# Two moves in a polysketch-attention and ELU-MLP kernel: a rounding step placed inside a division, and GpSimd's weight sums split over two steps

## The chip, the cores and the metric

The kernel runs on one core of one Trainium2 chip. The metric is device time in microseconds (us) of that core, lower is better. All numbers before the change come from three timed runs and from one more execution that the hardware profiler recorded.

## The reference, cut to what matters

Attention with a polynomial feature map feeds a two-layer block with an ELU between its layers.

```python
# q, k, v: (4, 4, 1088, 32); S1, S2: (8, 32); w_in: (128, 2048); w_out: (2048, 128)
def phi(x):                                   # 64 features from two sketches of 8
    a = einsum('rd,bhsd->bhsr', S1, x)
    b = einsum('rd,bhsd->bhsr', S2, x)
    return einsum('bhsi,bhsj->bhsij', a, b).reshape(..., 64)
kv  = einsum('bhsf,bhsd->bhfd', phi(k), v)
z   = sum(phi(k), axis=2)
num = einsum('bhsf,bhfd->bhsd', phi(q), kv)
den = einsum('bhsf,bhf->bhs', phi(q), z)[..., None] + 1e-06
x   = (num / den).transpose(0, 2, 1, 3).reshape(4352, 128)
h   = x @ w_in
g   = where(h > 0, h, exp(min(h, 0)) - 1)
out = g @ w_out
```

q, k and v arrive as 32-bit floats, S1, S2, w_in and w_out as 64-bit floats; of these the kernel reads each number as two 32-bit words and makes a 32-bit float itself.

## The kernel before, in words

**Tiling.** The 4352 rows of x are cut into 9 groups of at most 512 rows (`g`, 0 to 8; the last has 256). The 2048 hidden columns are cut into 8 blocks (`cp`, 0 to 7) of 256. One step is one pair (g, cp): TensorE multiplies block cp of w_in by the group (`mm1`), ScalarE and VectorE make the ELU of it in two halves (`elu`, tile `gg`), and two steps later TensorE multiplies the result by block cp of w_out. The list `steps` fixes the order: steps 0 to 13 go through groups 0 and 1 for the first blocks and end with blocks 6 and 7 of group 0; steps 14 and 15 are blocks 6 and 7 of group 1; from step 16 on, one group after another takes all eight blocks.

**Seven products instead of eight.** From step 14 on (`seven`), the product with w_out uses seven block products in place of eight. This needs sums of quarters of `gg` (`sums7`, tile `tt`, lines 751 to 756, four GpSimd instructions a step) and sums of quarters of w_out (`weights7`, tile `SS`, line 740, four GpSimd instructions for a range of blocks). `mm2_seven` (line 792) issues the matmuls; in each step its first products need `gg` alone, and the third kind, named `p6`, needs `tt` of line 755 and `SS`.

**The order of work** is written out by hand, engine by engine: each engine runs its instructions in the order of the program text. The lists `at`, `mid` and `late` put a piece of work into a step: after its `mm1`, between the two halves of the ELU, or at its end.

**Rounding of weights.** A block of weights goes through five steps: `RA` (line 101, VectorE, masks the upper word into `W`), `RB` (line 106, ScalarE), `RS` and `RM` (lines 116 and 120, VectorE), `RD` (line 128) and `RE` (line 136). `RA(0)` and `RA(1)` are the first steps for blocks 0 and 1 of w_in, whose data come by DMA from SyncE's queue (line 173).

**The first group's division.** Before the first step stands a start-up sequence. For group 0, `q2_den` computes the denominators and divides: a product (line 603, tile `pw`), a sum over eight terms (line 608, `den`), a reciprocal (line 609) and a product with it (line 611, `an`). Its argument `between` is a function that is called after the first of these. `q2_out` then forms the 64 features in two halves (line 624, `qp`), with `RA(1)` between them. TensorE transposes these halves (`q4_early`, line 636, `qtp`), and multiplies by kv (`q5_early`, line 643, `xps`); ScalarE copies the result to `xg` (line 649), on which the first `mm1` waits.

```python
    def q2_den(g, zq=None, between=None):
        ...
            nc.vector.tensor_mul(pw...)          # line 603
        if between:
            between()
        den = work.tile([P, 8 * H], F32, name="den", tag="den")
        nc.vector.tensor_reduce(den[:, :m], pw[:, :m], axis=AX, op=ADD)   # line 608
```

GpSimd at that time builds small tables for later groups (`make_Sxp`, `make_SWq`, `Z_share`: lines 312 to 318 and 454).

Of the kernel before, what the change touches and what calls it, by code (L numbers as in the profile page):

```python
# [22 lines left out]
def _ap(ap: bass.AP, free):  # L23
    return dataclasses.replace(ap, ap=[list(ap.ap[0])] + [list(x) for x in free])
# [3 lines left out]
def kernel(  # L28
# [28 lines left out]
    NP = NC // 2  # L57
# [120 lines left out]
    def round_w(f, i, *a):  # L178
        if wide:
            cp, w_in, w_out = order[i]  # L180
            c = slice(0 if w_in else 2 * P, 4 * P if w_out else 2 * P)
            f(raw_w[cp][:, c], W[:, cp, c], *a)

    def RA(i):
        round_w(round_a, i)
# [337 lines left out]
    def q1z_first():  # L523
        p = psum.tile([P, 512], F32, name="zqp", tag="h", bufs=4)
        for i in range(4):
            for u in range(2):
                b, t = half_tile(0, 2 * i + u)
                nc.tensor.matmul(p[64 * u:64 * u + 64, i * 32:i * 32 + 32].rearrange("p (h r) -> p h r", h=H),
                                 qT[b][:, t, :], SW[:, :, 2, :], skip_group_check=True, tile_position=(0, 64 * u))
        return p[:, :128].rearrange("p (t h r) -> p h t r", t=4, h=H)  # L530
# [65 lines left out]
    def q2_den(g, zq=None, between=None):  # L596
        m = H * (un[g] if g > 1 else qn[g])
        x = abw[g][:, :m, :]
        pw = pws[g % 2]
        if zq is None:  # L600
            nc.vector.tensor_mul(pw[:, :m, :R], x[:, :, R:2 * R], x[:, :, 2 * R:3 * R])
        else:
            nc.vector.tensor_mul(pw[:, :m, :R].rearrange("p (h t) r -> p h t r", h=H),
                                 x[:, :, R:2 * R].rearrange("p (h t) r -> p h t r", h=H), zq)
# [3 lines that stand above are left out]
        nc.vector.tensor_reduce(den[:, :m], pw[:, :m], axis=AX, op=ADD)  # L608
        nc.vector.reciprocal(den[:, :m], den[:, :m])
        an = work.tile([P, 8 * H, R], F32, name="an", tag="an")  # L610
        nc.vector.tensor_mul(an[:, :m], x[:, :, R:2 * R], _ap(den[:, :m], [[1, m], [0, R]]))
        ans[g] = an

    def q2_out(g, parts=1, between=None):
        m = H * qn[g]
        x, an = abw.pop(g), ans.pop(g)
        qp[g] = work.tile([P, 4 * H, R, R], F32, name="qp", tag="qp", bufs=2)
        for i in range(parts):
            if i and between:
                between()  # L620
            h = slice(i * m // parts, (i + 1) * m // parts)
            a_ = an[:, h]
            b_ = x[:, h, :R]
            nc.vector.tensor_mul(qp[g][:, h], _ap(a_, list(a_.ap[1:]) + [[0, R]]),
                                 _ap(b_, [b_.ap[1], [0, R], b_.ap[2]]))
# [337 lines left out]
    KO_first(7, KT)  # L963
    keep_warm(1, 96, 64)
    zq = q1z_first()
    q2_den(0, zq)
    RA(0)
    q2_out(0, 2, lambda: RA(1))
    KA(0)
    KS_first()  # L970
# [53 lines left out]
    def late(n, f, *a):  # L1024
        extra.setdefault((n, 1), []).append((f, *a))
# [75 lines left out]
    late(60, q4, 8)  # L1101

    late(12, weights7, slice(NP - 2, NP))
    late(15, weights7, slice(0, NP - 2))

    N = len(steps)
    for n in range(2, N):
# [95 lines left out]
```

## Time and profile before

| what | value |
|---|---|
| timed runs | 265.53, 265.70, 265.88 us; median 265.70 us |
| profiled execution, device time | 266.02 us |
| its span, first to last instruction | 264.2 us |
| TensorE busy | 258.6 us, 98% of the span |
| VectorE busy | 188.2 us, 71% |
| ScalarE busy | 184.5 us, 70% |
| GpSimd busy | 167.3 us, 63% |
| granted TensorE clock | full speed in all 40 slices |

The profile calls TensorE PE (its weight loads PEld), VectorE DVE, ScalarE ACT, GpSimd POOL and SyncE SP. L740 is line 740 of the kernel. Times are counted from the start of the span. Around the span lie 1.8 us that the profiled execution's device time has beyond it.

### The profile page before, as it was taken

The numbers are of one execution on the slowest core, as the hardware profiler recorded it, in microseconds if no ns is written. First come the engines' busy times: TensorE is split into PE (matmuls) and PEld (weight loads), VectorE is DVE, ScalarE is ACT, GpSimd is POOL, SyncE is SP. The second block draws the span as 40 slices with busy tenths as digits, with TensorE's granted clock in tenths as the row PEclk, the third lists the DMA queues.
The fourth block names the chain that finished last, engine by engine and source line by source line (L and its number), as shares of the span: only waits on it lengthen the run. The fifth ranks groups of instructions, "written<-read, shape, count | busy, mean of one in ns | idle before, by whom it ended". The sixth has DMA issues, their size and how long they took to land.

```text
span 264.2 us, 9735 instructions
## 1 busy us (share of the span) xinstructions
PE 258.6 (98%) x4127; PEld 160.7 (61%) x4127; DVE 188.2 (71%) x349; ACT 184.5 (70%) x356; POOL 167.3 (63%) x247
## 2 busy tenths in 40 slices
PE   8899999999999999999999999999999999999994
PEld 6652334354346666667666666665766666667994
DVE  6799999997969997996567675644446445674651
ACT  2469978677567556785587777776777777777792
POOL 4400009103279996798858799898688888997310
PEclk9999999999999999999999999999999999999999
DMA  6996089010011110001100110011001100110021
GB/s 183 342 347 200 0 254 241 12 55 35 2 22 25 23 24 2 2 4 20 28 3 0 26 20 0 2 15 29 3 2 20 23 4 0 17 17 10 2 32 30
DMA packets 26442, 13.73 MB, mean 52 GB/s; under 512 B 19328, under 2 KB 24576, under 8 KB 26400
## 3 DMA queue, kind: packets, MB, share of 16 engines
q1 hardware_dynamic: 25968, 12.76, 18.8%
q8 instruction: 32, 0.52, 0.9%
q10 hardware_dynamic: 368, 0.30, 0.3%
q14 instruction: 10, 0.08, 0.1%
q0 software_dynamic: 64, 0.07, 0.1%
HBM read 10.88 MB, written 2.23 MB: 50 GB/s over the span
## 4 chain that ended last, share of the span: by engine, by line
PE 96%; POOL 1%; DVE 1%; ACT 1%; issue 0%
PE h L257 44%; PE pb L792 16%; PE pa L792 13%; PE o L257 5%; PE pb L768 4%; PE ol L257 3%; PE idle L265 1%; PE kv L428 1%; PE h L686 1%; PE qps L686 1%; POOL kp L324 1%; PE kfps L360 1%; PE qps L576 1%; PE qtp L636 1%; PE kv L257 1%; PE abp L341 1%
## 5 line engine op out<-in xcount | busy, mean ns | idle before, releaser
L257 PE MATMUL h<-xg,W 128*32 128x512 f32 (+3 forms) x904 | 130.7, 539 | 0.3 <-ACT xg L649 0.3
L875 DVE SCALAR_TENSOR_TENSOR gg<-e,h 128x512 f32<-128x512 f32 x128 | 85.6, 682 | 54.1 <-ACT e L869 50.6
L867 ACT ACTIVATE e<-h 128x512 f32<-128x512 f32 x128 | 75.5, 590 | 45.8 <-PE h L257 44.0
L869 ACT ACTIVATE e<-e 128x512 f32<-128x512 f32 x128 | 80.9, 632 | 3.8
L257 PEld LDWEIGHTS h<-xg,W 128*32 128x32 f32 (+1 forms) x904 | 42.6, 122 | 43.1 <-issue 35.5
L754 POOL TENSOR_TENSOR tt<-gg 128x256 f32<-128x256 f32 x50 | 37.0, 741 | 15.3 <-DVE gg L875 14.9
L751 POOL TENSOR_TENSOR tt<-gg 128x256 f32<-128x256 f32 x50 | 36.7, 734 | 7.7 <-DVE gg L875 7.3
L755 POOL TENSOR_TENSOR tt<-tt,gg 128x256 f32<-128x256 f32 x50 | 37.5, 751 | 3.9
L756 POOL TENSOR_TENSOR tt<-gg,tt 128x256 f32<-128x256 f32 x50 | 37.2, 744 | 3.9
L792 PEld LDWEIGHTS pa<-gg,W 128*64 128x64 f32 (+1 forms) x496 | 23.8, 125 | 23.5 <-issue 22.9
L792 PE MATMUL pa<-gg,W 128*64 128x128 f32 (+1 forms) x496 | 30.5, 274 | 0.0
L792 PE MATMUL pb<-tt,SS 128*64 128x128 f32 (+1 forms) x480 | 29.5, 273 | 0.0
L792 PEld LDWEIGHTS pb<-tt,SS 128*64 128x64 f32 (+1 forms) x480 | 22.7, 126 | 0.0
L792 PE MATMUL pa<-tt,SS 128*32 128x128 f32 (+1 forms) x288 | 21.1, 273 | 0.0
L792 PE MATMUL pb<-gg,SS 128*64 128x128 f32 (+1 forms) x256 | 19.8, 273 | 0.0
L792 PE MATMUL pb<-tt,W 128*64 128x128 f32 (+1 forms) x256 | 19.8, 273 | 0.0
L133 POOL TENSOR_TENSOR raw<-raw,tiny 128x512 f32<-128x512 f32 x1 | 1.0, 1047 | 29.5 <-DVE raw L128 29.5
L257 PE MATMUL o<-gg,W 128*32 128x512 f32 x128 | 15.3, 594 | 0.0
L792 PEld LDWEIGHTS pa<-tt,SS 128*32 128x32 f32 (+1 forms) x288 | 13.5, 123 | 0.3 <-POOL tt L755 0.3
L792 PEld LDWEIGHTS pb<-gg,SS 128*64 128x64 f32 (+1 forms) x256 | 12.6, 125 | 0.0
L792 PEld LDWEIGHTS pb<-tt,W 128*64 128x64 f32 (+1 forms) x256 | 12.6, 125 | 0.0
L768 PE MATMUL pb<-gg,W 128*32 128x256 f32 x192 | 11.6, 380 | 0.0
(163 smaller groups left out, 279.5 us busy)
## 6 DMA issues: line engine op xcount, KB each, us to landing
raw<-in_moe_w_in_dram SPq DMA_DIRECT2D x8, 256.0 KB, 6.1
raw<-in_moe_w_out_dram SPq DMA_DIRECT2D x8, 256.0 KB, 6.0
hd_k<-in_k_dram SPq DMA_DIRECT2D x3, 544.0 KB, 7.2
hd_q<-in_q_dram SPq DMA_DIRECT2D x3, 544.0 KB, 8.6
out_dram<-ob SPq DMA_DIRECT2D x88, 16.0 KB, 1.5
v<-in_v_dram SPq DMA_DIRECT2D x4, 288.0 KB, 7.5
v<-in_v_dram SPq DMA_DIRECT2D x4, 256.0 KB, 8.4
hd_k<-in_k_dram SPq DMA_DIRECT2D x1, 288.0 KB, 3.3
```

What stands on the lines that cost most here:

```text
L257: nc.tensor.matmul(dst[c:c + tile], lhs[:, c:c + tile], rhs, skip_group_check=True, tile_position=(0, c), **kw)
L265: nc.tensor.matmul(idle[c:c + tile, :cols], ones[:, :tile], ones[:, :cols], skip_group_check=True, tile_position=(0, c))
L686: nc.tensor.matmul(ps[w][s * r:s * r + s, 64 * k:64 * (k + m)], lhs, qpT[g, i][rows, o + 2 * k:o + 2 * (k + m), f, :], start=(f == 0 and j ...
L751: nc.gpsimd.tensor_tensor(t[:, 0], b12, b11, op=SUB)
L754: nc.gpsimd.tensor_tensor(t[:, 2], b22, b12, op=SUB)
L755: nc.gpsimd.tensor_tensor(t[:, 1], t[:, 2], b11, op=ADD)
L756: nc.gpsimd.tensor_tensor(t[:, 3], b21, t[:, 1], op=SUB)
L768: nc.tensor.matmul(acc[1][0][r:r + width[0], 256 * hi:256 * hi + 256], lhs[:, w:w + width[0]], gg[:, c, 256 * u:256 * u + 256], start=(cp ...
L792: nc.tensor.matmul(bank[r:r + width[0], P * col:P * col + P], lhs[:, w:w + width[0]], rhs[:, u], start=(first and i in ((0,) if g == 1 els ...
L867: nc.scalar.activation(e, hs[g, cp][c][:, :n], RELU, scale=-1.0)
L869: nc.scalar.activation(e, e, EXP, scale=-1.0)
L875: nc.vector.scalar_tensor_tensor(gs[g, cp][:, c, :n], es[g, cp][:, c, :n], -1.0, hs[g, cp][c][:, :n], op0=ADD, op1=MAX)
```

## The change

The first step of rounding block 0 of w_in, `RA(0)`, is issued inside `q2_den` of group 0, between line 603 and line 608, in place of after line 611. The sums of w_out blocks 0 to 5, which were all made at the end of step 15, are made in two parts: blocks 0 to 2 at the end of step 13, and blocks 3 to 5 at the end of step 15. The values computed are the same.

```diff
     zq = q1z_first()
-    q2_den(0, zq)
-    RA(0)
+    q2_den(0, zq, lambda: RA(0))
     q2_out(0, 2, lambda: RA(1))
...
     late(12, weights7, slice(NP - 2, NP))
-    late(15, weights7, slice(0, NP - 2))
+    late(13, weights7, slice(0, 3))
+    late(15, weights7, slice(3, NP - 2))
```

## The prediction

> **What bounds the kernel now.** I read the busy shares first, then the chain that ended last.
>
> ```profile
> PE 258.6 (98%) x4127; PEld 160.7 (61%) x4127; DVE 188.2 (71%) x349; ACT 184.5 (70%) x356; POOL 167.3 (63%) x247
> PE 96%; POOL 1%; DVE 1%; ACT 1%; issue 0%
> ```
>
> TensorE carries 96% of the chain. An edit on VectorE or GpSimd can only shorten the start-up, before the first mm1 (16.1 us), or one of the few moments when TensorE waits later. So I looked for both. The chain in order of time, around the first step that uses w_out sums of block 0 (step 18 multiplies what step 16 made, group 2, block 0):
>
> ```profile
> 84.14 0.44 PE pa L792 x16
> 84.58 0.01 issue
> 84.59 0.43 PE pa L792 x8
> 85.02 0.87 PE pb L792 x32
> ```
>
> Columns: start, length, what. Eight such matmuls take 0.22 us elsewhere (0.44 for 16 in the first line), and these took 0.43: the 56 of the step took 1.75 us from 84.14 to 85.89, against 1.53 us in the step before (80.89 to 82.42). TensorE stood for **0.2 us**. The table of waits names the releaser (total us, times, longest):
>
> ```profile
> PEld pa L792 <- POOL tt L755: 0.3, 1, 0.3
> ```
>
> GpSimd's own order of time shows why it was late:
>
> ```profile
> 64.66 0.46 POOL L740 TENSOR_TENSOR SS<-W,SS 128x128 f32<-128x128 f32 x1
> 69.75 0.73 POOL L751 TENSOR_TENSOR tt<-gg 128x256 f32<-128x256 f32 x1 [4.62 <-DVE gg L875]
> ...
> 78.29 1.02 POOL L740 TENSOR_TENSOR SS<-W 128x384 f32<-128x384 f32 x1
> 79.39 1.01 POOL L740 TENSOR_TENSOR SS<-SS,W 128x384 f32<-128x384 f32 x1
> 80.35 1.02 POOL L740 TENSOR_TENSOR SS<-W 128x384 f32<-128x384 f32 x1
> 81.33 1.01 POOL L740 TENSOR_TENSOR SS<-W,SS 128x384 f32<-128x384 f32 x1
> 82.31 0.73 POOL L751 TENSOR_TENSOR tt<-gg 128x256 f32<-128x256 f32 x1
> 83.00 0.72 POOL L754 TENSOR_TENSOR tt<-gg 128x256 f32<-128x256 f32 x1
> 83.80 0.73 POOL L755 TENSOR_TENSOR tt<-tt,gg 128x256 f32<-128x256 f32 x1
> ```
>
> The four w_out sums hold GpSimd from 78.29 to 82.31. The ELU that line 751 reads was there at 78.06 (VectorE, 77.37 + 0.69), and its second half at 79.21. Line 755 ends at 84.53; TensorE goes on at 84.59. Before, GpSimd had 4.6 idle us, from 65.1 to 69.75.
>
> In the start-up, VectorE's order of time:
>
> ```profile
> 10.12 0.29 DVE L603 TENSOR_TENSOR pw<-abq,zqp 128x128 f32<-128x128 f32 x1 [0.23 <-PE zqp L528]
> 10.51 0.30 DVE L608 TENSOR_REDUCE den<-pw 128x16 f32<-128x144 f32 x1
> 10.84 0.25 DVE L609 RECIPROCAL den<-den 128x16 f32<-128x16 f32 x1
> 11.13 0.29 DVE L611 TENSOR_TENSOR an<-abq,den 128x128 f32<-128x128 f32 x1
> 11.34 0.29 DVE L101 TENSOR_SCALAR W<-raw 128x256 uint32<-128x256 uint32 x1
> 11.54 0.68 DVE L624 TENSOR_TENSOR qp<-an,abq 128x512 f32<-128x512 f32 x1
> 12.14 0.28 DVE L101 TENSOR_SCALAR W<-raw 128x256 uint32<-128x256 uint32 x1
> 12.34 0.68 DVE L624 TENSOR_TENSOR qp<-an,abq 128x512 f32<-128x512 f32 x1
> ```
>
> An instruction that needs the one ahead starts about 0.03 us after its end (10.81 to 10.84); one that doesn't starts before that end (11.34 against 11.42). The second half of qp releases TensorE (transposes at 13.17, 0.14 us after), and the chain then runs through PE and ACT to mm1 without a gap. So what VectorE gains here counts in full.
>
> **What the Trainium skill says.** "SBUF — State Buffer", section "Who interferes with whom": VectorE and GpSimd share a pair of SBUF ports under an exclusive lock. A tensor_scalar in its two-port mode takes it, a VectorE instruction with two SBUF inputs contends with a GpSimd one that reads, a reduce never does; the later one waits out the earlier. The trace agrees: at 45.72 line 120 took 2.07 us instead of 0.43, ending 0.29 after GpSimd's line 324 ended (47.50); at 43.99 line 116, two inputs, took 1.69 instead of 0.69. "VectorE: DVE Perf Modes", section "Mode 2×_2P": tensor_scalar gets two results a cycle even on 32-bit data. Line 101 agrees: 0.29 us for 256 elements, 0.43 for 512, so 0.55 ns an element, against 1.05 for two-input products (0.29 for 128, 0.68 for 512). RA(0) is thus an instruction that takes the lock.
>
> **Part 1, RA(0) into the division.** Removed between lines 611 and 624: their starts are 0.41 us apart. In group 2, without a step between, they are 0.32 apart (67.52 to 67.84), so the gain is 0.09. Added between 603 and 608: group 1 already has such a step there (RA(2)), and its starts are 16.20, 16.40 and 16.60, that is 0.40 apart; group 0 shows 0.39 today without it. The cost is 0.01. Net on paper **-0.08 us**.
>
> The lock takes part of it back. RA(0) will start near 10.33. GpSimd then runs the four copies of line 318 (9.85 to 10.51) and line 454 (10.46 to 10.68); at 11.34 it was idle. The nearest row is line 109 at 2.95: a tiny tensor_scalar beside GpSimd's copy of line 269 took 0.29 instead of 0.17 and ended 0.04 after the copy (3.20). With the rest of 256 elements at 0.55 ns, RA(0) held by the last copy ends at 10.51 + 0.04 + 0.12 = 10.67 instead of 10.62: +0.05. Bounds: 0 if it gets in first; if line 454 gets in first, 10.68 + 0.16 = 10.84, +0.22. I take +0.05, as line 116 got the lock between two GpSimd instructions (45.1). Part 1: **-0.03 us**, between -0.08 and +0.14.
>
> RA(0) also waits for its DMA. That was issued at 3.89 and landed 5.4 us later, at 9.3, 1.0 us before the new place: no wait. If the data came after 10.33, line 608 and all of the division behind it would wait that long. RB(0) on ACT gains nothing: it stands behind the copy at 11.89. No DMA is moved, and SP's queue keeps its order.
>
> **Part 2, the split sums.** One block is 64 columns. A line-740 instruction takes 0.46 us for 128 columns and 1.02 for 384, so about 0.60 for 192. By start-to-start times, interpolated, the four take 0.68 + 0.55 + 0.55 + 0.57 = 2.35 us (the 384-wide ones take 4.02). Four instructions are added in all: GpSimd does 0.7 us more. At the end of step 13 its first four run from 65.12, behind the sums of blocks 6 and 7, to about 67.5; nothing of GpSimd is queued behind them until line 751 at 69.75. Cost nothing, covered by the idle 4.6 us; without that cover it would be 2.35 us of GpSimd.
>
> At the end of step 15, GpSimd is free at 78.29 + 2.35 = 80.64 instead of 82.31, and line 755 ends near 82.9. TensorE wants it at 84.39 (its first 16 products start at 83.95 and take 0.44). The stall of **0.2 us goes**, with 1.5 us to spare. What is late next: line 755 for the following step ended at 87.56, wanted at 89.2, so nothing. From 82.4 to 102 TensorE is busy 19.59 of 19.60 us, and the steps there take 1.53 to 1.56 us apart from the switches after other matmuls: no second stall to win.
>
> The lock again: lines 601 (66.58), 611 (67.52) and 666 (67.84) of group 2's division have two SBUF inputs and now meet GpSimd. Line 601 falls into the third sum and may wait 0.3, line 611 perhaps 0.1; by 67.9 GpSimd is through. Line 673, which follows, ends at 70.82, and TensorE takes its result at 71.75: 0.93 us of slack covers it.
>
> **Sum.** -0.20 - 0.03 = -0.23 us on the profiled execution (span 264.2, device time 266.02; the 1.8 around it unchanged). That execution lies 0.32 above the median; from the median 265.70 it gives **265.5 us** (265.47), or -0.09%. A measurement of this kernel can tell about 0.2%, 0.53 us, from no change; so I forecast no change that counts.
>
> **Rivals.** (a) *The stall is larger without the profiler, or in most executions.* One more lock lost by GpSimd before 84.5 costs it what line 755 lost at 92.92 (1.60 instead of 0.73), near 0.8 us, and then the sum of the gains is 0.2 + 0.8 + 0.03 = 1.0: 264.7. For it: GpSimd is busy without a gap from 78 to 102. Against: in this stretch VectorE has one SBUF input in nearly everything, and all three runs agree within 0.35 us. (b) *Slower: group 2's division is held by the new sums.* If each of lines 601, 611 and 666 waits out a whole sum of 0.60, the transposed features come 1.8 us late, beyond the slack of 0.93, which is the point from which it decides; TensorE stands 0.87 us before its line 686 at 71.75, and the total is 265.70 - 0.23 + 0.87 = 266.3. Against: only four sums exist, and they end by 67.9. A w_in block that lands late would show earlier, at 10.33, at a like price. (c) *Part 1 does nothing or loses 0.14, part 2 as said*: 265.6. That the moves don't take place at all is excluded by in-order queues.
>
> **How the numbers follow.** Forecast and (c) together 0.68, all within 0.2%; (a) 0.2; (b) 0.12. Faster by over 0.2%: 0.2; within: 0.68; slower: 0.12. The range for 8 in 10 goes from 265.0, which takes in (a) where half of the 0.8 us was lost (265.07), to 265.95, where (c) with an ordinary spread of runs ends.
>
> **What would show it.** Right: in the chain, the third line-792 group of step 18 takes 0.22, the wait on line 755 is gone, GpSimd starts line 751 of group 2 near 80.6, line 740 has eight 192-wide instructions in place of four 384-wide ones, line 608 starts between 10.5 and 10.6, and line 624 near 11.5. Wrong: a wait of PE at line 686 near 71.8, line 101 at 10.33 longer than 0.4, or line 608 after 10.7.

## The result, and the profile after

| | before | after |
|---|---|---|
| median of 22 timed runs each | 265.69 us | 265.38 us |
| lowest to highest | 265.31 to 266.26 | 265.08 to 265.79 |
| profiled execution's span | 264.2 us | 263.3 us |

The ratio is 0.9988, with a 95% interval from 0.9983 to 0.9994: 0.31 us less, between 0.16 and 0.45. That is a small gain, clear of noise as the interval does not reach 1, and under the 0.2% named in the prediction. The forecast was -0.23 us and 265.5 us.

The page's first line and the chain's share by engine are as they were; TensorE still carries the time:

```profile
PE 257.8 (98%) x4127; PEld 160.5 (61%) x4127; DVE 188.2 (71%) x349; ACT 184.5 (70%) x356; POOL 168.2 (64%) x251
PE 96%; POOL 1%; DVE 1%; ACT 1%; issue 0%
```

POOL has four instructions and 0.9 us more (0.7 forecast). The chain in order of time (start, length, what), at step 18:

```profile
83.63 0.66 PE pa L792 x24
84.29 0.87 PE pb L792 x32
```

The 24 products of bank pa now run as one piece in 0.66 us; before, they took 0.44 + 0.01 + 0.43. From 83.63 to 85.16, where the next h begins, are 1.53 us instead of 1.75: the stall of **0.22 us** is gone, and no wait of PE on POOL is left in the table of waits. GpSimd's own order of time shows what moved (start, length, line, operation):

```profile
64.59 0.60 POOL L740 TENSOR_TENSOR SS<-W 128x192 f32<-128x192 f32 x1
...
66.38 0.64 POOL L740 TENSOR_TENSOR SS<-W,SS 128x192 f32<-128x192 f32 x1
69.45 0.73 POOL L751 TENSOR_TENSOR tt<-gg 128x256 f32<-128x256 f32 x1 [2.43 <-DVE gg L875]
...
77.79 0.59 POOL L740 TENSOR_TENSOR SS<-W 128x192 f32<-128x192 f32 x1
...
79.57 0.60 POOL L740 TENSOR_TENSOR SS<-W,SS 128x192 f32<-128x192 f32 x1
80.12 0.75 POOL L751 TENSOR_TENSOR tt<-gg 128x256 f32<-128x256 f32 x1
...
81.65 0.74 POOL L755 TENSOR_TENSOR tt<-tt,gg 128x256 f32<-128x256 f32 x1
```

The first four sums end at 67.02 and leave 2.43 idle us; the second four take 2.33 us (77.79 to 80.12) instead of 4.02. Line 755 ends at 82.39. TensorE's own order of time (which counts a start a little earlier than the chain does) shows when it is wanted:

```profile
83.45 0.62 PE L792 MATMUL pa<-gg,W 128*32 128x128 f32 x16
83.89 0.40 PE L792 MATMUL pa<-tt,SS 128*32 128x128 f32 x8
```

The products with `tt` start at 83.89, 0.44 us after the 16 ahead of them, so without a wait: 1.5 us to spare. Before, the same two groups started at 83.95 and 84.59, 0.64 us apart.

VectorE's order of time in the start-up:

```profile
9.62 0.29 DVE L603 TENSOR_TENSOR pw<-abq,zqp 128x128 f32<-128x128 f32 x1 [0.23 <-PE zqp L528]
9.82 0.33 DVE L101 TENSOR_SCALAR W<-raw 128x256 uint32<-128x256 uint32 x1
10.07 0.29 DVE L608 TENSOR_REDUCE den<-pw 128x16 f32<-128x144 f32 x1
10.39 0.25 DVE L609 RECIPROCAL den<-den 128x16 f32<-128x16 f32 x1
10.68 0.29 DVE L611 TENSOR_TENSOR an<-abq,den 128x128 f32<-128x128 f32 x1
11.01 0.69 DVE L624 TENSOR_TENSOR qp<-an,abq 128x512 f32<-128x512 f32 x1
11.62 0.29 DVE L101 TENSOR_SCALAR W<-raw 128x256 uint32<-128x256 uint32 x1
11.82 0.69 DVE L624 TENSOR_TENSOR qp<-an,abq 128x512 f32<-128x512 f32 x1
```

Everything stands 0.5 us earlier than before, but so does line 603, which nothing in the change precedes. Counted from the start of line 603, the first half of line 624 starts after 1.39 us (before: 1.42), the second after 2.20 (2.22), and mm1 after 5.96 (5.98; it starts at 15.58, before at 16.10). **Part 1 gives 0.02 to 0.03 us.** RA(0) took 0.33 us, 0.04 more than in its old place. GpSimd's order of time at that moment:

```profile
9.35 0.66 POOL L318 COPY SWq<-Sxp 128x32 f32<-128x32 f32 x4
9.96 0.27 POOL L454 TENSOR_TENSOR SWq<-SW 128x16 f32<-128x16 f32 x1
```

The last of the four copies runs from 9.79 to 10.00. RA(0) ends 0.14 us after it, ahead of line 454, which took 0.22 us in the kernel before and takes 0.27 here.

TensorE's last products end 0.72 us earlier in the second profile (259.93 instead of 260.65). Of these, 0.50 lie ahead of line 603; the other 0.23 (both rounded) lie behind it and are the change's. In the six profiles with the same code up to there (these two and four of the experiments below), line 603 started anywhere from 9.62 to 10.24. In the profile of before, the S matrices' first rounding started at 2.52 (it waits for its DMA), in that of after at 2.33. So two profiled executions of this kernel can't be compared by their ends; they are compared from the start of line 603.

### The profile page after: what moved, and what is told of

It reads as the page before. It is cut to its first block, busy times and chain, and to the rows that moved or that the text cites. A ratio compares the mean times of both kernels' runs of the same rounds, so it can differ in the third digit from the quotient of the medians.

```text
span 263.3 us, 9739 instructions
## 1 busy us (share of the span) xinstructions
PE 257.8 (98%) x4127; PEld 160.5 (61%) x4127; DVE 188.2 (71%) x349; ACT 184.5 (70%) x356; POOL 168.2 (64%) x251
## 4 chain that ended last, share of the span: by engine, by line
PE 96%; POOL 1%; DVE 1%; ACT 1%; issue 0%
PE h L257 44%; PE pb L792 16%; PE pa L792 13%; PE o L257 5%; PE pb L768 4%; PE ol L257 3%; PE idle L265 1%; PE kv L428 1%; PE h L686 1%; PE qps L686 1%; POOL kp L324 1%; PE kfps L360 1%; PE qps L576 1%; PE qtp L636 1%; PE kv L257 1%; PE abp L341 1%
```

## The experiments

Timed runs are compared with runs of the kernel before on the same chip; each interval is 95%. The experiments ran on three chips, and the changed kernel was not timed again on them; where a text says "above the changed kernel's median", that median is the 265.38 us of the first table, and a difference of a tenth of a us from it means nothing. The edits of the first two are shown against the kernel before, the others against the changed kernel if nothing else is said.

**Part 1 alone.**

```diff
-    q2_den(0, zq)
-    RA(0)
+    q2_den(0, zq, lambda: RA(0))
```

> Part 1 alone: RA(0) inside group 0's division, the w_out sums all at the end of step 15 as before. Theory (the stall of step 18 gives nearly all of the gain; RA(0) gives 0.02 to 0.03 us): time within 0.1 us of before, -0.03 us; in the trace line 624 starts 1.39 us after line 603 (before: 1.42), line 101 takes about 0.33 us, and the third group of line 792 in step 18 still takes 0.43 us. Rival (RA(0) gives the larger share, 0.2 us or more, as the cheaper place counts in full): -0.2 us, line 624 1.2 us after line 603.

Measured: 265.51 against 265.61 us, ratio 0.9996 (0.9988 to 1.0005), so no change that the timed runs can tell. In the trace line 624 starts 1.38 us after line 603, line 101 takes 0.32 us, and the stall is still there. The chain at step 18:

```profile
83.84 0.44 PE pa L792 x16
84.28 0.03 issue
84.30 0.43 PE pa L792 x8
84.73 0.87 PE pb L792 x32
```

The rival, a gain of 0.2 us from RA(0), falls by the trace, as line 624 would have had to start after 1.2 us; the interval of the timed runs still takes it in. RA(0) met another instruction here: the copies had ended (at 10.07) before it began at 10.08, and it ended 0.15 us after line 454 (10.03 to 10.25), which kept its 0.22 us.

**Part 2 alone.**

```diff
-    late(15, weights7, slice(0, NP - 2))
+    late(13, weights7, slice(0, 3))
+    late(15, weights7, slice(3, NP - 2))
```

> Part 2 alone: the w_out sums split over steps 13 and 15, RA(0) in its old place after line 611. Theory: -0.20 to -0.22 us against before, the same as the whole change within 0.1 us; the 56 matmuls of step 18 take 1.53 us instead of 1.75, no wait on line 755. Rival (the stall removed is given back later, at another wait on tt or at group 2's division): within 0.05 us of before, with a new wait of TensorE between 64 and 100 us.

Measured: 265.42 against 265.61 us, ratio 0.9994 (0.9986 to 1.0002). The middle is where it was expected, but the interval reaches no change; the timed runs alone do not prove it. The chain at step 18 has the stall gone:

```profile
84.24 0.66 PE pa L792 x24
84.89 0.88 PE pb L792 x32
```

But the rival had forecast a new wait of TensorE before 100 us, and this profile has one, among the products of line 428 (tile `kv`):

```profile
88.57 0.05 PE kv L428 x2
88.62 0.13 issue
88.75 0.23 PE kv L428
```

The last of these is one product, and such a product takes about 0.02 us elsewhere: TensorE stood 0.33 us there. From line 603 to its last product this execution was no shorter than the one before (250.5 us both). It took 265.94 us, 0.5 above the median of its kernel, so it doesn't stand for the others. The same product stood as long in the profile of the late w_in block, 0.16 us in that of the doubled sums, 0.06 in the last one below, and not at all in that of the changed kernel or in the six others. The profile names no engine or DMA for it ("issue"), and its cause stays open. It is seen only where the sums are split, in four of eight such profiles and in none of the three others; the 22 timed runs of the whole change, which show a gain, speak against a loss of this kind in most executions.

**More GpSimd work at the place of the stall.**

```diff
     late(15, weights7, slice(3, NP - 2))
+    late(15, weights7, slice(3, NP - 2))
```

> The change, with the sums of blocks 3 to 5 made twice in a row at the end of step 15: 2.35 us more of GpSimd. In the changed kernel line 755 of group 2, block 0 ends 1.5 us before TensorE wants it. Theory (the wait on tt in step 18 is the only thing that the GpSimd queue costs there): TensorE stands 2.35 - 1.5 = 0.85 us in step 18 and the time rises by 0.85 us over the changed kernel, +0.55 us against before. Rival (GpSimd catches up through other idle time, or the wait is hidden): no more than +0.3 us over the changed kernel. Second rival (the delay runs on through the following steps as GpSimd is busy without a gap): over +1.5 us.

Measured: 266.27 against 265.61 us, ratio 1.0021 (1.0010 to 1.0032): +0.66 us, or 0.89 above the changed kernel's median, where 0.85 was expected. The table of waits (total, times, longest):

```profile
PEld pa L792 <- POOL tt L755: 1.0, 1, 1.0
```

TensorE's order of time:

```profile
83.46 0.62 PE L792 MATMUL pa<-gg,W 128*32 128x128 f32 x16
84.78 0.43 PE L792 MATMUL pa<-tt,SS 128*32 128x128 f32 x8 [0.70 <-POOL tt L755]
```

The 16 products from 83.46 fill 0.44 us, to 83.90; the next starts at 84.78, so TensorE stood 0.88 us. There is one such wait and not two: line 755 was in time again at the next step. The margin of 1.5 us is real, and at this one dose what GpSimd did beyond it (2.36 us more, so 0.86) came back as time of the kernel.

**All six blocks at step 13.** This is rival (b) of the prediction with twice the sums at that place. In group 2, lines 601, 611 and 666 are the division and the features, line 673 transposes these on VectorE, and line 686 is TensorE's first product with them.

```diff
-    late(13, weights7, slice(0, 3))
-    late(15, weights7, slice(3, NP - 2))
+    late(13, weights7, slice(0, NP - 2))
```

> The change with all six blocks of w_out sums at the end of step 13, none at step 15 (four 384-wide instructions from about 64.6 to 68.6 us instead of four 192-wide ones). It puts the GpSimd reads on top of group 2's division. Theory of the port lock with 0.9 us of slack: line 601 is held for about 0.5 us and line 611 for up to 0.9, the transposed features (line 673) come 1.0 to 1.5 us later than in the changed kernel, and TensorE stands 0.1 to 0.6 us ahead of line 686 of group 2: the time is 0.1 to 0.6 us above the changed kernel's, so between -0.2 and +0.3 us against before. Rival (nothing of the division is near TensorE): the same as the changed kernel, -0.3 us.

Measured: 265.91 against 265.61 us, ratio 1.0011 (1.0004 to 1.0017): +0.30, at the upper end of what was expected. VectorE's order of time in the kernel before, then here with two of GpSimd's sums, and then the chain:

```profile
66.58 0.27 DVE L601 TENSOR_TENSOR pw<-abw 128x128 f32<-128x128 f32 x1
67.52 0.29 DVE L611 TENSOR_TENSOR an<-abw,den 128x128 f32<-128x128 f32 x1
67.84 1.23 DVE L666 TENSOR_TENSOR qp<-an,abw 128x1024 f32<-128x1024 f32 x1
```

```profile
65.66 1.01 POOL L740 TENSOR_TENSOR SS<-SS,W 128x384 f32<-128x384 f32 x1
67.65 1.06 POOL L740 TENSOR_TENSOR SS<-W,SS 128x384 f32<-128x384 f32 x1
66.07 0.75 DVE L601 TENSOR_TENSOR pw<-abw 128x128 f32<-128x128 f32 x1
67.48 0.35 DVE L611 TENSOR_TENSOR an<-abw,den 128x128 f32<-128x128 f32 x1
67.87 1.92 DVE L666 TENSOR_TENSOR qp<-an,abw 128x1024 f32<-128x1024 f32 x1
```

```profile
70.31 1.24 DVE qpT L673
71.55 0.14 issue
71.69 0.67 PE qps L686 x8
```

Lines 601, 611 and 666 took 0.48, 0.06 and 0.69 us more than in the kernel before: lines 601 and 666 each ended only after the sum that was running when they started (66.67 and 68.71), while line 611 lost almost nothing. The chain now leads through line 673 of VectorE, and the table of waits has a wait of PE on it of 0.4 us. At step 18 TensorE is 0.4 us later than in the changed kernel (84.07 against 83.63, line 603 having started within 0.03 us). Another 0.2 us is lost at 119 us, in products of line 428 again and without a named cause; together 0.6 us in the trace, where its median lies 0.5 above the changed kernel's. With three blocks at step 13 only line 601 was held, by 0.2 us. Rival (b) is thus a real mechanism; with the sums split the delay stays within the slack of 0.93 us, and with all of them moved it doesn't.

**A quiet GpSimd for RA(0), first try.**

```diff
-    late(2, make_SWq)
-    late(3, Z_share, 0)
+    late(6, make_SWq)
+    late(6, Z_share, 0)
```

> The change, with GpSimd's table copies (lines 316 and 318) and line 454 moved from the start-up into the end of step 6, so that GpSimd is idle when RA(0) runs inside the division. Theory (RA(0) is held by the port lock of GpSimd's copy for 0.04 us): line 101 takes 0.29 us instead of 0.33, line 624 starts 1.34 to 1.36 us after line 603 instead of 1.39, and the time falls by 0.04 us, too little for the timed runs to tell. Rival (the 0.33 us is a chance of the profile and not the lock): no change of line 101.

Measured: line 101 took 0.29 us and line 624 started 1.35 us after line 603, as the expectation from the lock had it. But the time was 265.92 against 265.59 us, ratio 1.0011 (1.0005 to 1.0018): 0.3 slower, which the expectation had not foreseen. GpSimd's order of time, then line 116 (a rounding step of VectorE) in the kernel before and here:

```profile
42.16 0.15 POOL L316 MEMSET SWq<- 128x64 f32 x1
42.24 0.86 POOL L318 COPY SWq<-Sxp 128x32 f32<-128x32 f32 x4
43.06 0.22 POOL L454 TENSOR_TENSOR SWq<-SW 128x16 f32<-128x16 f32 x1
43.24 4.78 POOL L324 TENSOR_TENSOR kp<-abk 128x1280 f32<-128x1280 f32 x2
```

```profile
43.99 1.69 DVE L116 SCALAR_TENSOR_TENSOR W<-raw,W 128x512 uint32<-128x512 uint32 x1
43.70 2.51 DVE L116 SCALAR_TENSOR_TENSOR W<-raw,W 128x512 uint32<-128x512 uint32 x1
```

The table of waits:

```profile
PE h L257 <- DVE gg L875: 0.4, 1, 0.4
```

The small instructions stand ahead of line 324, a long product of GpSimd in two parts, which starts 2.33 us after the start of line 134 (40.91), the GpSimd instruction ahead of them, instead of 1.27; line 116, held until the first part of 324 ends, takes 2.51 us (before: 1.69), and the ELU behind it comes late enough for TensorE to wait. From there on TensorE is 0.6 us later than in the changed kernel.

**Second try, behind line 324.** The edit is against the first try.

```diff
-    late(6, make_SWq)
-    late(6, Z_share, 0)
+    late(9, make_SWq)
+    late(9, Z_share, 0)
```

> The change, with lines 316, 318 and 454 on GpSimd moved from the start-up to the end of step 9, behind both halves of line 324 (at the end of step 6 they stood ahead of them). Theory (at step 6 they held up line 324, which held lines 116 and 120 on VectorE by the port lock until TensorE ran dry near 50 us; behind line 324 GpSimd is idle until 62 us): line 324 starts near 42.0 to 42.6 again, line 116 takes 1.7 us and not 2.5, no wait of TensorE near 50 us; line 101 inside the division still takes 0.29 us; the time is 0.04 us under the changed kernel's, -0.3 to -0.35 us against before. Rival (the loss at step 6 came from something else in the move, as the absence of GpSimd work in the start-up): +0.3 us against before again.

Measured: line 116 takes 1.72 us, PE does not wait near 50 us, line 101 in the division takes 0.28 us. The time is 265.38 against 265.58 us, ratio 0.9996 (0.9988 to 1.0004). The median is the changed kernel's; the 0.04 us expected are too little to be seen. The rival's +0.3 us is outside the interval.

**The first w_in block lands later.**

```diff
-    load_w(0, 0)
     load_hd(nc.sync, "q", q, 0, 8, NT)
     load_w(1, 0)
+    load_w(0, 0)
     load_w(1, 1)
```

> The change, with the first w_in block's DMA issued after those of the second q part and of w_in block 1 (they were after it). It should land where block 1's did, near 10.8 to 11.1 us instead of 9.3 to 9.6. Theory (VectorE's queue is in order, so a late block stands in front of the whole division): RA(0), ready at 9.8 to 10.3, starts only at the landing, line 608 and all behind it come 0.6 to 1.2 us later, and the time rises by 0.5 to 1.2 us over the changed kernel. In the old place, 11.3 us, the same landing would have cost nothing. Rival (the data wait is covered by other work): no more than 0.2 us.

Measured: 266.24 against 265.59 us, ratio 1.0029 (1.0019 to 1.0039): +0.65, or 0.86 above the changed kernel's median. VectorE's order of time:

```profile
11.77 0.29 DVE L101 TENSOR_SCALAR W<-raw 128x256 uint32<-128x256 uint32 x1 [1.46 <-DMA raw<-in_moe_w_in_dram]
```

RA(0) waited 1.46 us, until 11.77, later than the 11.1 expected, and line 624 started 2.9 us after line 603 instead of 1.39. This profiled execution took 267.33 us and was among the slowest of the 19 (265.77 to 267.43), so its wait is longer than the one behind the median. The new place makes the division depend on a DMA that before had until 11.3. Whether the old place would have cost nothing, as the expectation says, was not run; a landing near 11.7, as here, would have been late for it too.

**RA(1) moved too.**

```diff
-    load_hd(nc.sync, "q", q, 0, 8, NT)
     load_w(1, 0)
+    load_hd(nc.sync, "q", q, 0, 8, NT)
...
-    q2_out(0, 2, lambda: RA(1))
+    RA(1)
+    q2_out(0, 2)
```

It was run with the table copies at step 6 and at step 9.

> The change; beside it RA(1) moved from between the two halves of line 624 to just ahead of the first (behind line 611, where RA(0) was before), the table copies moved to step 6 as in the other kernel, and w_in block 1's DMA issued ahead of the second q part, so that it has landed by then. Theory (a step in a dependency gap costs 0.09 us, between independent halves 0.20): the second half of line 624 ends 0.11 us earlier for RA(1), 0.04 for the lock, so 0.15 us earlier from line 603 on (2.05 us from the start of line 603 to the start of the second half, instead of 2.20), mm1 starts as much earlier, and the time falls by 0.15 us against the changed kernel, -0.4 to -0.45 against before. Rival (another input of mm1, the rounding of w_in or the q transpose, is late next): less than 0.05 us.

> RA(1) ahead of both halves of line 624, w_in block 1's DMA ahead of the second q part, and the GpSimd table copies at the end of step 9. Theory: mm1 starts 5.80 us after the start of line 603 (the changed kernel 5.96), no wait near 50 us, and the time falls by 0.15 us against the changed kernel: -0.45 us against before, 0.9983. Rival (what is won in the start-up is lost at a later wait): within 0.1 us of the changed kernel, -0.3 us against before.

Measured at step 6: 265.98 against 265.59 us, ratio 1.0008 (1.0001 to 1.0015). In the trace the start-up was faster as expected (mm1 5.79 us after line 603), but the copies' loss near 50 us was there too. The timed runs show no gain over the first try, which has the same copies at step 6 and RA(1) in its old place (265.92 us). At step 9: 265.20 against 265.58 us, ratio **0.9986** (0.9979 to 0.9992). VectorE's order of time at step 9:

```profile
10.77 0.29 DVE L611 TENSOR_TENSOR an<-abq,den 128x128 f32<-128x128 f32 x1
10.98 0.28 DVE L101 TENSOR_SCALAR W<-raw 128x256 uint32<-128x256 uint32 x1
11.18 1.29 DVE L624 TENSOR_TENSOR qp<-an,abq 128x512 f32<-128x512 f32 x2
```

The two halves run without a step between them, the second starts 2.04 us after line 603 (9.75) instead of 2.20, and mm1 starts 5.78 us after it instead of 5.96. So -0.37 us against before by the timed runs (-0.45 expected), and mm1 0.18 earlier than in the changed kernel by the trace. The second try, with the same copies and timed on the same chip, has 265.38 us. It is the version with the lowest median; its interval overlaps with the changed kernel's, and the order of the DMAs was not varied alone.

## Why the prediction was right, point by point

- **The stall of 0.2 us at step 18**: right in place, size and cause. It measured 0.22, part 1 alone kept it, part 2 alone removed it, and the doubled sums brought it back with the size that the 1.5 us margin gives. One argument beside it does not carry: TensorE's 19.59 busy us of 19.60 between 82.4 and 102 were to show that no second stall is there, but that stretch holds the stall of 0.2 us itself, which the view thus can't show. The even step times of 1.53 to 1.56 us are the argument.
- **The price of the sums**: 0.60 us for 192 columns, four in 2.35; measured 0.60, and 2.33 and 2.43. Line 740's two widths in the trace were enough to interpolate.
- **Part 1, -0.08 on paper and 0.05 back by the lock**: measured -0.03 at the first half of line 624. RA(0) lost 0.04 to GpSimd, and it takes 0.28 to 0.29 us when GpSimd is idle. In the profile after, the case taken applied: RA(0) got in between the last copy and line 454. In that of part 1 alone it waited out line 454, the case of the upper bound, and lost only 0.03, as line 454 was nearly done. Neither case came near the bound of +0.14, and which of them comes is a matter of a tenth of a us. The timed runs can't tell part 1 from nothing; the trace can.
- **The cover of the first sums**: right in outcome. Line 601 was held 0.2 us (0.3 forecast), line 611 not at all (0.1 forecast).
- **The DMA's margin of 1.0 us was mis-sized.** In the profile after, the block's DMA was issued at 3.90 and landed 5.7 us later, at 9.6, and RA(0) started at 9.82: 0.2 us. The prediction took the landing and VectorE's start times from one execution, while line 603 alone moves by 0.6 us between executions. In the five other profiles with RA(0) in the new place and the DMA order kept, the margin was about 0.2 to 0.9 us. The change stands nearer to the late-landing case than was said. That no wait showed in any of them is right in outcome and in part luck.
- **The sum**: -0.23 forecast, -0.23 in the traces from line 603 on, -0.31 (-0.45 to -0.16) by the timed runs. Whether the 0.08 between them is more than spread, these runs don't tell. Rival (a), a gain of 1.0 us from a larger stall than the profile's, is out: it lies far beyond the interval.
- **A slip**: the two-input products shown (0.29 us for 128 elements, 0.68 for 512) give 1.02 ns an element and not 1.05. Nothing rests on it.

## What to carry to other kernels

In a kernel whose main engine is busy for 98% of the time, look in the chain for the few pieces that take longer than their like; each can be the gain of one edit, and the helper engine's order of time around it shows how much margin an edit must make. Before work is moved into another engine's idle time, check both ends: which instructions there share its port, and what is queued behind it (six small table instructions cost 0.5 us ahead of one long instruction, and behind it nothing that the timed runs could tell). Here a rounding step used as filler, where the next instruction has to wait for the one ahead anyway, cost 0.02 us between lines 603 and 608 (with GpSimd idle) and 0.09 between 611 and 624, and between independent instructions 0.20; but it brings its own waits to the front of the queue.

## What the runs showed of the hardware

A VectorE instruction held by the port lock gets in between two GpSimd instructions that follow each other. RA(0) got in between the last copy and line 454 and lost 0.04 us; line 116 of the kernel before ended at 45.68, 0.55 us after the first part of line 324 (1280 columns), while the second part ran on to 47.50. In the runs with all sums at step 13 and with the copies at step 6 the loss therefore follows what is left of the one GpSimd instruction in progress: line 666, which started 0.84 us before the end of a sum, lost 0.69 us, and RA(0), beside instructions of 0.2 us, lost 0.03 to 0.04.

GpSimd pays too: the second part of line 324 (1024 columns), in which line 116 ran, took 2.41 us, against 1.96 for the same shape in the start-up of the kernel before (at 7.62), and the four copies of line 318 took 0.66 us in the start-up and 1.32 us at step 9, where VectorE's lines 120 to 136 ran beside them.
